# Constant matmuls in TensorE's early gaps, v loads moved forward, and a different order of ScalarE's first work

## The chip, the cores and the metric

The kernel runs on one core of one Trainium2 chip. The metric is device time in microseconds (us) of one execution. The kernel before takes 507.7 us (median); its four executions lie between 507.67 and 508.16 us. Engines: TensorE (PE; its weight loads are PEld), VectorE (DVE), ScalarE (ACT), GpSimd (POOL) and SyncE (SP), which issues the DMA transfers here.

## The reference, cut to what matters

```python
def _attn_ref(q, k, v, f_logit):                # (4, 8, 768, 48) each
    f = 1.0 / (1.0 + np.exp(-f_logit))
    for t in range(S):                          # a gated recurrence
        state = f[:, :, t, :, None] * state + np.einsum('bhd,bhe->bhde', k[:, :, t], v[:, :, t])
        y[:, :, t] = np.einsum('bhd,bhde->bhe', q[:, :, t], state)

def _moe_ref(x, w1, w2, w3, w_out):             # x: 3072 x 384
    a = x @ w1; b = x @ w2                      # 384 -> 1024
    h = a * b @ w3                              # 1024 -> 1024
    return (h @ w_out).astype(np.float32)       # 1024 -> 384
```

The output of the recurrence is the input x of the feed-forward part. Weights arrive as 64-bit floats.

## The kernel before

The recurrence is done in 24 chunks of 128 steps, four to a block of 512 rows. A chunk needs its gates (ACT), two scans and two products (DVE), a transpose, scores, values and a state update (PE), copies out of PSUM (ACT) and a mask (GpSimd). w3 and w_out are folded into one matrix on the chip ("folds", eight of them), and every weight is converted from 64-bit words to f32 by ACT and DVE.

The order of instructions on each engine is fixed when the program is built, by a plan: each task has a cost in us and a lag, and a list scheduler takes whatever can start first. Each engine's list is then fixed in that order.

```python
    def moves(issue, size, rate, emit, deps, prio):
        i = plan.add("SP", issue, emit, deps, prio, lag=0.6)
        return plan.add("DMA", size / rate, lambda: None, [i], prio, lag=1.3)
    # ... in attention(u), chunk u
        t["lf"] = moves(0.87, 197, 250, load(fu, f_logit), free(2, "g"), n0 - 30)
        t["lk"] = moves(0.87, 197, 250, load(ku, k), free(2, "k"), n0 - 29.5)
        t["lq"] = moves(0.87, 197, 250, load(qu, q), free(3, "q"), n0 - 29)

        def load_v():
            s["v"] = loads.tile([P, DM], F32, name="vt")     # pool "loads": 3 buffers
            nc.sync.dma_start(s["v"], v[u])

        t["lv"] = moves(0.45, 197, 320, load_v, past(u, 3, "v", "s"), n0 - 27)
    # ... in fetch(): a load of weights (1 MB) and its conversion
        ld = moves(0.45, total, 380, load, held[-2:], prio)
        # ACT: magnitude, rest; DVE: shifted (clamp, then shift), signed, joined
    # ... at the end
    for t in plan.order():
        t["emit"]()
```

There are three buffers for v: v of chunk u can be loaded only when chunk u - 3 has been used (`past(u, 3, "v", "s")`).

Of the kernel before, what the change touches and what calls it, by code (L numbers as in the profile page):

```python
# [36 lines left out]
F32 = mybir.dt.float32  # L37
# [8 lines left out]
P = 128  # L46
# [9 lines left out]
TB = 512  # L56
# [4 lines left out]
NPE = 4  # L61
# [3 lines left out]
TH = TB // 2  # L65
KH = KF // 2
LOW = float.fromhex("0x1p-15")
HIGH = float.fromhex("0x1.dffffep+16")
FLOOR = 2.0**-60
RANGE = 2.0**-40  # L70

# [53 lines left out]
@with_exitstack  # L125
def kernel(
    ctx: ExitStack,
    tc: tile.TileContext,
    q: bass.AP,
    k: bass.AP,  # L130
    f_logit: bass.AP,
    v: bass.AP,
    w1: bass.AP,
    w2: bass.AP,
    w3: bass.AP,
    w_out: bass.AP,
    leaf_mask: bass.AP,
    out: bass.AP,
):
    nc = tc.nc  # L140
    const = ctx.enter_context(tc.tile_pool(name="const", bufs=1))
    ident = const.tile([P, P], F32, name="ident")
    w12 = const.tile([P, 2, KM, DFF], F32, name="w12")
    wc = const.tile([P, KF, DM], F32, name="wc")
    left = const.tile([1, 1], I32, name="left")
    with tc.manual_schedule():
        outside = ranged(tc, q, k, f_logit, v, w1, w2, w3, w_out, out, ident, w12, wc, left)
        with tc.If(outside > 0, preferred_fallthrough_block=True, label="general"):
            general(tc, q, k, f_logit, v, leaf_mask, out, ident, w12, wc)
# [24 lines left out]
def ranged(ctx, tc, q, k, f_logit, v, w1, w2, w3, w_out, out, ident, w12, wc, left):  # L174

    nc = tc.nc
# [11 lines left out]
    ps_f = ctx.enter_context(tc.tile_pool(name="ps_f", bufs=NF, space=PSUM))  # L188

    floor = keep.tile([R, NQ], F32, name="floor")  # L190
# [35 lines left out]
    plan = Plan()  # L226
# [3 lines left out]
    moving = plan.add("PE", 0.0, lambda: None, takes=["ab"], prio=-1e9)  # L230
    coming = plan.add("PE", 0.0, lambda: None, takes=["ab"], prio=-1e9)

    def heads(t):
        return t.rearrange("p (h c) -> p h c", c=C)

    def setup():
        nc.scalar.activation(warm, nc.const_aps.tensor(0.0, (R, 1), F32), AF.Sigmoid)
        for i in range(2):
            nc.gpsimd.memset(fs[i][32:64], 30.0)  # L239
            nc.gpsimd.memset(ks[i][32:64], 0.0)  # L240
            nc.gpsimd.memset(qs[i][32:64], 0.0)
            if i == 0:
                make_identity(nc, ident)
        nc.gpsimd.memset(early[32:64, 2:4], 30.0)
        nc.gpsimd.memset(early[32:64, 0:2], 0.0)
        nc.gpsimd.memset(qs[2][32:64], 0.0)
        nc.gpsimd.memset(qs[3][32:64], 0.0)
        nc.vector.memset(floor, FLOOR)
        nc.vector.memset(heads(floor)[:, :, 0], 1.0)
        nc.vector.memset(back, 0.0)  # L250
        for t in gate:
            nc.vector.memset(t[:, NQ : NQ + 1], 0.0)
        nc.vector.memset(ones, 1.0)
        for t in sb:
            nc.vector.memset(t, 0.0)

        nc.gpsimd.memset(perm, 0.0)
        for i, (kc, hp) in enumerate(met):
            for par in range(2):
                for r, t, at_, n in runs(2 * hp + par):  # L260
                    if t == kc:
                        a = 64 * par + at_
                        nc.gpsimd.tensor_copy(perm[:, i, r : r + n], ident[0:R, a : a + n])
# [16 lines left out]
    def need(u):  # L280
        return (0.0, 1.0, 2.0, 3.0)[u] if u < 4 else 45.0 + 14.5 * (u - 4)

    def past(u, n, *names):
        return [tk[u - n][nm] for nm in names if u >= n and nm in tk[u - n]]

    def moves(issue, size, rate, emit, deps, prio):

        i = plan.add("SP", issue, emit, deps, prio, lag=0.6)
        return plan.add("DMA", size / rate, lambda: None, [i], prio, lag=1.3)

    def attention(u):
        s, t = st[u], tk[u]
        opens, closes = u % NCH == 0, u % NCH == NCH - 1
        n0 = need(u)
# [9 lines left out]
        def free(n, *names):  # L304
# [3 lines left out]
            return asked[4:5] + [tk[u - n if u - n >= 4 else u % n][nm] for nm in names]  # L308
# [6 lines that stand above are left out]
            s["v"] = loads.tile([P, DM], F32, name="vt")  # L315
            nc.sync.dma_start(s["v"], v[u])

        t["lv"] = moves(0.45, 197, 320, load_v, past(u, 3, "v", "s"), n0 - 27)

        def gates():  # L320
            nc.scalar.activation(gate[u % 2][:, 0:NQ], fu, AF.Sigmoid)  # L321
# [11 lines left out]
        def last():  # L333
            nc.scalar.copy(lasts[:, u], heads(s["P"])[:, :, C - 1])
# [3 lines left out]
        def ends():  # L338
            nc.vector.reciprocal(heads(back)[:, :, C - 1], heads(s["P"])[:, :, C - 1])
# [151 lines left out]
        n = u // UB  # L491
# [379 lines left out]
    def fetch(loads_, a, prio, subs, deps=()):  # L871





        total = subs[-1][1]
        if not wide:
            def plain():
                for place_, src in loads_:  # L880
                    for c0, c1, dst, _, _ in subs:
                        d = dst().rearrange("p (a m) -> p a m", a=a)
                        m = (c1 - c0) // a
                        b0 = c0 // a if len(subs) > 1 else 0
                        nc.sync.dma_start(d[place_], src[:, :, b0 : b0 + m])
            waits = [d for sub in subs for d in sub[4]]
            ld = plan.add("SP", 1.9 * total / 512, plain, waits, prio, lag=2.0)
            return [ld] * len(subs)
        load_no = len(users)
        buf = load_no if load_no < len(raws) else (load_no - len(raws)) % NRAW  # L890
        raw = raws[buf][:, 0 : 2 * total]
        words = raw.rearrange("p (n two) -> p n two", two=2)
        held = [g for no, b_, gs in users if b_ == buf for g in gs]

        def load():
            for place_, src in loads_:
                nc.sync.dma_start(raw.rearrange("p (a m) -> p a m", a=a)[place_], src.bitcast(U32))

        ld = moves(0.45, total, 380, load, held[-2:], prio)
        asked.append(ld)  # L900
        got = []
        users.append((load_no, buf, got))
        ends = []

        def sub(c0, c1, dst, due, waits):
            n = c1 - c0
            w = n / 512
            lo, hi = words[:, c0:c1, 0], words[:, c0:c1, 1]
            a0 = spot[0] if n <= 512 else (spot[0] + 512) // 1024 * 1024 % 2048
            spot[0] = (a0 + (512 if n <= 512 else 1024)) % 2048  # L910
            m = magnitudes[:, a0 : a0 + n]
            mine = range(a0 // 512, (a0 + n + 511) // 512)
            s = {}

            def magnitude():
                nc.scalar.activation(m, hi.bitcast(F32), AF.Abs)  # L916

            def rest():
                nc.scalar.activation(lo.bitcast(F32), lo, AF.Copy, bias=2.0, scale=2.0**-51)  # L919

            def shifted():
                nc.vector.tensor_scalar(m, m, HIGH, LOW, ALU.min, ALU.max)
                nc.vector.tensor_scalar(m.bitcast(U32), m.bitcast(U32), 3, None, ALU.logical_shift_left)

            def signed():
                s["to"] = dst()
                nc.vector.scalar_tensor_tensor(
                    s["to"].bitcast(U32), hi, 0x80000000, lo, ALU.bitwise_and, ALU.bitwise_or
                )

            def joined():
                to = s["to"].bitcast(I32)
                nc.vector.tensor_tensor(to, m.bitcast(I32), to, ALU.add)  # L933

            past = [joins[i] for i in mine if i in joins]
            b = plan.add("ACT", 0.2 + 0.43 * w, magnitude, [ld] + past, due)
            e = plan.add("ACT", 0.2 + 0.43 * w, rest, [ld], due)
            h = plan.add("DVE", 0.32 + 0.54 * w, shifted, [b], due)
            g = plan.add("DVE", 0.16 + 0.53 * w, signed, [e, b] + list(waits), due)
            j = plan.add("DVE", 0.16 + 0.53 * w, joined, [h, g], due - 1)  # L940
            parts.append((g, j))
            joins.update({i: j for i in mine})
            got.append(g)
            ends.append(j)

        for one_ in subs:
            sub(*one_)
        return ends
# [104 lines left out]
    for u in range(NU):  # L1053
        attention(u)
        if u == 3:
            weights()
        if u == NU - 1:
            judged = plan.add("DVE", 1.5, judge, [tk[i]["y"] for i in range(NU)], -20)
        if u % UB == UB - 1:
            ffn(u // UB)  # L1060
    for t in plan.order():
        t["emit"]()
    return blk[NB - 1]["outside"]

# [336 lines left out]
```

## Time and profile before

| | before |
|---|---|
| time, median (range) | 507.69 us (507.67 to 508.16) |
| span of the profiled run | 506.3 us |
| PE busy | 488.8 us, 97% |
| DVE busy, 25 to 60 us | 33.58 of 35 us |
| first feed-forward matmul on PE | 37.07 us |
| second fold on PE | 90.22 us |

PE is full after the start, and DVE nearly full until 150 us. The lines are in the prediction. A "w3 row" is below one block of w3 after its conversion, which the fold of the same number on PE needs; its last step is a DVE instruction (line 933).

### The profile page before, as it was taken

What the parts mean: (1) busy time and instruction counts of PE and PEld (TensorE: products, weight loads), DVE (VectorE), ACT (ScalarE), POOL (GpSimd) and SP (SyncE); (2) the same over time, 40 slices, a digit from 0 to 9 for tenths busy, and PEclk for the clock granted to TensorE, in tenths of its full rate; (3) what the DMA queues carried; (4) which work ended last, traced back from release to release, by engine and by line L of the source; (5) the groups of instructions that cost most, each with busy time, mean ns of one, the idle gap of its engine ahead of it and who ended that gap; (6) DMA issues with size and microseconds to landing.
All of it is one profiled execution on the core that took longest, in us unless ns stands there. A gap on an engine that the chain in (4) does not pass through costs nothing.

```text
span 506.3 us, 8806 instructions
## 1 busy us (share of the span) xinstructions
PE 488.8 (97%) x3346; PEld 409.2 (81%) x3346; DVE 362.4 (72%) x701; ACT 162.1 (32%) x340; POOL 42.7 (8%) x51
## 2 busy tenths in 40 slices
PE   2899999999999999999999999999999999999995
PEld 2788854666688887889888899888899888889994
DVE  6799999999998769866677766256564677564541
ACT  4589454854434345222332112321010011011000
POOL 8120010001101201001110000110000000000000
PEclk9999999999999999999999999999999999999999
DMA  6959466762222265311160001210002100000011
GB/s 177 363 206 305 135 216 220 251 199 79 61 79 84 67 190 161 96 34 45 45 193 16 1 6 31 59 50 0 2 21 61 45 1 0 1 0 1 32 49 52
DMA packets 30163, 46.02 MB, mean 91 GB/s; under 512 B 6560, under 2 KB 20384, under 8 KB 28320
## 3 DMA queue, kind: packets, MB, share of 16 engines
q1 hardware_dynamic: 30112, 45.38, 28.5%
q8 instruction: 28, 0.46, 0.4%
q14 instruction: 23, 0.19, 0.1%
HBM read 36.70 MB, written 4.72 MB: 82 GB/s over the span
## 4 chain that ended last, share of the span: by engine, by line
PE 94%; POOL 2%; DVE 2%; DMA 1%; issue 0%; ACT 0%; SPq 0%; DVEq 0%; POOLq 0%; ACTq 0%
PE f L530 68%; PE f L984 8%; PE pa L370 5%; PE pa L420 4%; PE pk L456 2%; PE pk L396 2%; PE pa L435 2%; DMA vt<-in_v_dram 1%; PE f L509 1%; PE f L420 1%; PE f L428 1%; DVE fwd L329 0%; POOL A L385 0%; DVE bwd L351 0%; POOL f L239 0%
## 5 line engine op out<-in xcount | busy, mean ns | idle before, releaser
L530 PE MATMUL f<-xt,w 128*128 128x256 f32 (+1 forms) x600 | 160.1, 398 | 0.1
L530 PEld LDWEIGHTS f<-xt,w 128*128 128x128 f32 x600 | 113.0, 190 | 24.5 <-issue 9.5
L530 PE MATMUL f<-place 128*128 128x192 f32 (+1 forms) x504 | 114.0, 352 | 0.0
L530 PEld LDWEIGHTS f<-place 128*128 128x128 f32 x504 | 87.3, 190 | 6.8 <-issue 1.1
L385 POOL TENSOR_SCALAR_AFFINE_SELECT A<-A 128x1024 f32<-128x1024 f32 x24 | 31.4, 1309 | 294.2 <-ACT A L379 294.2
L984 PE MATMUL f<-place 128*128 128x384 f32 x128 | 43.1, 491 | 0.0
L633 ACT COPY a<-f 128x256 f32<-128x256 f32 x36 | 13.4, 372 | 75.5 <-PE f L530 59.7
L530 PE MATMUL f<-xt,place 128*128 128x256 f32 x144 | 37.2, 381 | 0.0
L984 PEld LDWEIGHTS f<-place 128*128 128x128 f32 x128 | 23.8, 190 | 15.8 <-issue 0.5
L530 PE MATMUL f<-wc,ab 128*128 128x192 f32 x192 | 35.7, 329 | 0.0
L530 PEld LDWEIGHTS f<-wc,ab 128*128 128x128 f32 x192 | 31.8, 190 | 0.9
L657 DVE TENSOR_TENSOR place<-f,a 128x256 f32<-128x256 f32 x36 | 15.2, 423 | 23.7 <-PE f L530 23.6
L329 DVE TENSOR_TENSOR_SCAN fwd<-gate,floor 112x512 f32<-112x512 f32 x24 | 30.2, 1258 | 2.6 <-ACT gate L321 1.7
L379 ACT COPY A<-pa 128x1024 f32<-128x1024 f32 x24 | 24.2, 1009 | 22.7 <-PE pa L370 22.7
L370 PEld LDWEIGHTS pa<-Q,K 48*128 48x128 f32 x384 | 24.9, 199 | 6.9 <-issue 4.7
L351 DVE TENSOR_TENSOR_SCAN bwd<-gate,back 112x512 f32<-112x512 f32 x24 | 29.8, 1240 | 0.8
L530 PEld LDWEIGHTS f<-xt,place 128*128 128x128 f32 x144 | 26.9, 189 | 3.8 <-DVE place L657 0.2
L370 PE MATMUL pa<-Q,K 48*128 48x128 f32 x384 | 29.7, 298 | 0.0
L485 ACT ACTIVATE ys<-pa 112x512 f32<-112x512 f32 x20 | 11.9, 597 | 40.8 <-PE pa L435 20.5
L919 ACT ACTIVATE place<-place 128x512 f32<-128x512 uint32 (+2 forms) x24 | 21.1, 890 | 8.0 <-DMA place<-in_w_out_dram 4.8
L916 ACT ACTIVATE place<-place 128x512 f32<-128x512 f32 (+2 forms) x24 | 21.2, 884 | 4.1 <-DVE w L933 2.1
L420 PEld LDWEIGHTS pa<-A,vt 128*48 128x48 f32 (+1 forms) x320 | 17.4, 130 | 6.2 <-issue 4.8
(104 smaller groups left out, 623.0 us busy)
## 6 DMA issues: line engine op xcount, KB each, us to landing
place<-in_w_dram SPq DMA_DIRECT2D x14, 1024.0 KB, 5.5
vt<-in_v_dram SPq DMA_DIRECT2D x24, 192.0 KB, 3.0
out_dram<-o SPq DMA_DIRECT2D x24, 192.0 KB, 2.1
q<-in_q_dram SPq DMA_DIRECT2D x46, 96.0 KB, 2.5
f<-in_f_logit_dram SPq DMA_DIRECT2D x44, 96.0 KB, 2.4
k<-in_k_dram SPq DMA_DIRECT2D x44, 96.0 KB, 2.4
place<-in_w_out_dram SPq DMA_DIRECT2D x4, 768.0 KB, 5.5
xt<-ys SPq DMA_DIRECT2D x120, 24.0 KB, 1.8
```

The source lines that it names most:

```text
L329: nc.vector.tensor_tensor_scan(s["P"], gate[u % 2][:, 0:NQ], floor, 0.0, ALU.mult, ALU.max)
L351: nc.vector.tensor_tensor_scan(s["R"][:, ::-1], gate[u % 2][:, NQ:0:-1], back[:, ::-1], 0.0, ALU.mult, ALU.max)
L370: nc.tensor.matmul(s["pa"][:, par, cols], lhsT=s["K"][rows(par), cols], rhs=s["Q"][rows(par), cols], start=True, stop=True,)
L379: nc.scalar.copy(s["A"].rearrange("p r h c -> p r (h c)"), s["pa"])
L385: nc.gpsimd.affine_select(out=a, in_=a, pattern=[[0, H], [1, C]], compare_op=ALU.is_ge, fill=0.0, base=0, channel_multiplier=-1,)
L420: nc.tensor.matmul(y_block(b)[64 * half : 64 * half + w], lhsT=s["v"][:, h * D : h * D + w], rhs=s["A"][:, par, hp], start=bank not in met ...
L530: nc.tensor.matmul(out_, lhsT=lhs[i], rhs=rhs[i], start=start and i == 0, stop=i == len(lhs) - 1, skip_group_check=True,)
L633: nc.scalar.copy(q["a"], q["X"])
L657: nc.vector.tensor_tensor(ups["u3", k], q["Y"], q["a"], ALU.add)
L916: nc.scalar.activation(m, hi.bitcast(F32), AF.Abs)
L919: nc.scalar.activation(lo.bitcast(F32), lo, AF.Copy, bias=2.0, scale=2.0**-51)
L984: nc.tensor.matmul(w3s["p", jc], lhsT=w3s[jc][:, kc * P : kc * P + P], rhs=wos[:, kc], start=(kc == 0), stop=(kc == KF - 1),)
```

## The change

The intent: TensorE runs its first matmuls slowly (the scores of a chunk take 2.01 us at 17 us and 1.11 us at 26 us), so let it multiply constants from the second microsecond on and in every planned gap up to 35 us; issue v of the first four chunks (NPE is 4) ahead of later chunks' loads; and tell the plan that the first weight loads land later, so that it puts ScalarE's chunk work ahead of conversions.

```diff
+FULL = 35.0
@@
+    def idle(n):
+
+        to = ps_f.tile([P, TB], F32, name="f")[:, 0:TH]
+        for _ in range(n):
+            nc.tensor.matmul(to, lhsT=floor[:, 0:P], rhs=floor[:, 0:TH], start=True, stop=True)
+
+    plan.add("PE", 7.8, lambda: idle(9), prio=-1e8)
@@
-    def moves(issue, size, rate, emit, deps, prio):
+    def moves(issue, size, rate, emit, deps, prio, late=0.0):
@@
-        return plan.add("DMA", size / rate, lambda: None, [i], prio, lag=1.3)
+        return plan.add("DMA", size / rate, lambda: None, [i], prio, lag=1.3 + late)
@@
-        t["lv"] = moves(0.45, 197, 320, load_v, past(u, 3, "v", "s"), n0 - 27)
+        t["lv"] = moves(0.45, 197, 320, load_v, past(u, 3, "v", "s"), n0 - (28.2 if u < NPE else 27))
@@
-        ld = moves(0.45, total, 380, load, held[-2:], prio)
+        ld = moves(0.45, total, 380, load, held[-2:], prio, max(0.0, 5.5 - 1.5 * load_no))
@@
+    ready_at = 0.0
     for t in plan.order():
+        if t["eng"] == "PE" and t["at"] < FULL:
+            n = int((t["at"] - ready_at) / 0.43)
+            if ready_at and n:
+                idle(n)
+            ready_at = t["end"]
         t["emit"]()
```

## The prediction

> **What bounds the kernel now.** I read the page's first two parts, then the chain of work that ended last for the first 70 us, then stretches of 20 us, then the timeline of single engines.
>
> The page says that TensorE (PE) is the bound, and where it is not:
>
> ```profile
> PE 488.8 (97%) x3346; PEld 409.2 (81%) x3346; DVE 362.4 (72%) x701; ACT 162.1 (32%) x340; POOL 42.7 (8%) x51
> ...
> PE   2899999999999999999999999999999999999995
> ...
> DVE  6799999999998769866677766256564677564541
> ...
> PEclk9999999999999999999999999999999999999999
> ```
>
> PE is idle for 506.3 - 488.8 = 17.5 us, and most of that lies in the first slice (12.7 us long). VectorE (DVE) is at nine tenths or more from the third slice to the twelfth, so in the first 150 us it is nearly as full as PE. The clock row shows nothing, yet the durations do. The chain at the start:
>
> ```profile
> 8.78 3.04 DMA vt<-in_v_dram
> ...
> 14.38 0.98 PE pk L396 x4
> 15.36 1.90 PE f L420 x15
> 17.26 2.01 PE pa L370 x16
> 19.27 1.02 PE pk L456 x14
> 20.29 2.86 PE f L509 x12
> ...
> 25.70 1.11 PE pa L370 x16
> ```
>
> The same sixteen matmuls of line 370 (scores of one chunk) take 2.01 us at 17.26 and 1.11 us at 25.70; the twelve of line 509 take 2.86 us here and 1.60 us at 32.48. Everything on PE before about 22.8 us runs at half speed, and from 14.38 us on PE is the chain without a gap. Before that the chain is the v load of the first chunk, issued at 8.78 us and landed at 11.82 us. By stretches:
>
> ```profile
> 0.00:20.00 20.00, 9.67 (x88) 8.20 (x88) 13.78 (x25) 8.42 (x17) 12.33 (x28) 1.00 0.73 229
> 20.00:40.00 20.00, 19.68 (x203) 17.64 (x202) 19.00 (x33) 16.87 (x35) 4.19 (x3) 1.00 0.72 264
> 40.00:60.00 20.00, 20.00 (x88) 16.49 (x87) 19.03 (x40) 13.90 (x28) 0.00 (x0) 1.00 0.65 218
> 60.00:80.00 20.00, 20.00 (x111) 10.81 (x110) 19.30 (x29) 11.24 (x17) 1.42 (x1) 1.00 0.59 191
> 80.00:100.00 20.00, 20.00 (x99) 11.51 (x98) 19.61 (x23) 13.27 (x18) 1.25 (x1) 1.00 0.76 259
> ```
>
> Columns: busy time of PE, weight loads, DVE, ScalarE, GpSimd; clock; DMA. After the start PE loses nearly nothing (20.00 of 20). So the end moves by what PE saves in the first 23 us, unless DVE, at 19.0 to 19.6 of 20, cannot deliver earlier. One place shows how tight that is. DVE finishes the second w3 row and PE uses it in the fold at once:
>
> ```profile
> 88.54 1.23 DVE L933 CUSTOM_DVE_ANT_0 place<-place 128x2048 uint16<-128x2048 uint16 x1
> ```
>
> ```profile
> 90.22 5.43 PE L984 MATMUL f<-place 128*128 128x384 f32 x16
> ```
>
> Ready at 89.77, used at 90.22: 0.45 us of slack. By the same reading the later folds have 2.7 to 6.0 us (third: ready 94.48, used 97.19; eighth: ready 126.6, used 132.6).
>
> [...] here full speed came about 8.4 us after PE became continuous at 14.38. [...] the 128x512 operation of line 922 takes 0.42 us, but 1.31 us where it meets GpSimd's select at 28.5 us.
>
> **The change part by part.**
>
> *Nine constant matmuls at the start.* Each is f32, 128x256, which the machine runs as two passes; a pass takes about 0.215 us at full clock (22 to 23 of them fill 5 us between 45 and 50 us), so 0.43 us for the pair and 0.86 us at half clock. They need only the constant tile "floor", set at 1.60 us, so they start near 1.7 us. [...] The first real work, the transposes of line 396, starts at 8.48 us. So they cost nothing, or up to about 1 us if the clock stays low (9 x 0.86 = 7.7, end 9.4).
>
> *Fillers in planned gaps up to 35 us.* [...] the number is the planned gap over 0.43 rounded down, so if the plan is right they fit in gaps. Where the real work is ready sooner than planned, each costs up to 0.43 us. They also draw PSUM buffers from the pool of five that the plan does not count, a possible small wait.
>
> *What the clock is worth on PE.* Slow minus fast duration by group: first transposes 0.98-0.55, scores 2.08-1.16, update 1.06-0.67, second transposes 0.98-0.55, values 1.97-1.09, second scores 2.08-1.16, second update 1.09-0.67, joining matmuls 2.93-1.60: 0.43+0.92+0.39+0.43+0.88+0.92+0.42+1.33 = 5.7 us, of which 4.0 us lie after 14.38, on the gapless chain. The gaps of PE between 8.4 and 14.35 are a further 5.95-4.05 = 1.9 us.
>
> *v of the first chunk earlier.* In the order of priorities v of chunk 0 moves from behind chunk 2's loads to behind chunk 1's k: three pairs of loads (q of 1, f and k of 2), each 0.84 us on the queue, so its issue moves from 8.78 to about 6.1 us and it lands near 9.1. The update of chunk 0 then waits for its transposes (about 9.7 us), not for v at 11.82. The loads overtaken move by 0.42 us each and were early.
>
> *What both give DVE.* In the first 25 us DVE waits 1.19 us at 13.07 (state of chunk 0, after the late v) and 1.84 us at 20.34 (state of chunk 1, after slow PE). Both go: 3.0 us. Two operations inflated by GpSimd there (0.89 for 0.69, 0.96 for 0.36) may move out of the collision or not, 0.8 us.
>
> *ScalarE's order.* The plan now believes the first four weight loads land 5.5, 4.0, 2.5 and 1.0 us later, so chunk work precedes conversions. In the trace the state copy of chunk 1 is ready at 21.69 but starts at 23.56, behind two conversions and a copy that waited for slow PE. Worth about 1 us to the chunks, paid by conversions started later; zero in sum, I think, since DVE is the limit for conversions.
>
> *Sum.* PE could start its unbroken feed-forward work up to 5.7 + 1.9 = 7.6 us sooner. But it then runs into DVE: at the second fold PE can be ahead only by DVE's own gain plus 0.45 us, that is 3.0 + 0.45 = 3.5 us; later folds have slack. I choose the smaller bound and take off 0.2 us for fillers in the way: 3.3 us. 507.7 - 3.3 = 504.4 us.
>
> **The rivals.** *The full gain.* If the rearranged plan finds other PE work while the second w3 row is awaited, or puts that row ahead of chunk 5 on DVE (4.5 us of work just before it, 81.46 to 86.0), PE keeps more, perhaps 5 to 6 us: 502. For it: slack of 2.7 us and more at all later folds. Against: the priorities of that stretch are unchanged. *DVE and weight loads give nothing.* The 5 MB of weights queued from 13.45 us keep the DMA engines at a share of 0.95 to 1.02 from 15 to 25 us, and conversions are put off; if the feed-forward start stays near 37 us because the third w1 piece is still converted at 36.1, the PE time saved turns into idle time and fillers: 506.5 to 507.5. Against: that piece had been held up by DVE, not by its load. *The fillers harm.* Warming runs on, or fillers delay the first chunks by 1 to 2 us, or a PSUM buffer wait appears: up to 508.5. For it: the plan's clock is not the chip's. Against: PE has 8.4 us with nothing to do.
>
> **Range and chances.** The centre is the DVE-bound sum, the low end most of the full gain, the high end most of the absorbed one: 504.4 us, 502.0 to 506.5. A 2% change is 10.2 us, above the 7.6 us that is to be had at most, so faster by over 2% has 0.01. Slower by over 2% needs a disturbed plan far beyond the first 35 us: 0.01. Within 2%: 0.98.
>
> **What would show it right or wrong.** Right: scores of line 370 at about 1.1 us already for chunk 0 or 1; first v landed by 9.5 us; the two DVE waits gone; the first feed-forward matmul of line 530 several us before 37.07; the second fold 3 to 3.5 us before 90.22, with PE's idle time or a DVE wait just ahead of it; the rest of the trace shifted by that amount. Wrong: slow matmuls still after 10 us (the constants do not raise the clock), transposes starting after 8.5 us (fillers in the way), the feed-forward start unmoved, or the second fold moved by more than 4 us (DVE no bound) or less than 2.5 us (a new wait before it). A shift that shrinks after 140 us would mean that later waits, not the start, set the end.

## The result, and the profile after

The changed kernel takes 514.38 us (median of 4 runs, 512.67 to 514.99), the kernel before 507.72 in the same rounds. Ratio 1.0124, 95% interval 1.0097 to 1.0151. Ratios here and below are the mean time of one kernel's fast runs over that of the other's fast runs of the same rounds, so not quite the ratio of the medians. The change makes the kernel 1.2% slower, where 0.7% faster was predicted; the span of the profiled run grew from 506.3 to 510.6 us. The profiled run is the fastest of the changed kernel's four (512.67 us, granted clock 0.995; the others 513.84 to 514.99 us with 0.990 to 0.992). So the profile accounts for 4.3 us of the loss; the further 1.2 to 2.3 us of the other runs go with a lower clock, and no profile of them was kept.

The first part works as meant. PE's timeline of the changed kernel (start, duration, instruction, count; in later lines brackets give the idle time just before and what ended it):

```profile
8.48 0.57 PE L405 MATMUL pk<-ident,K 112*128 112x112 f32 x4
9.02 1.16 PE L379 MATMUL pa<-Q,K 48*128 48x128 f32 x16
10.11 0.67 PE L465 MATMUL pk<-vt,kt 128*64 128x48 f32 x16
```

The first transposes start at 8.48 us as before, but at full speed (0.57 us for 0.98; the nine constants before them are 18 matmuls in the trace, from 1.66 to 8.43 us), and the update of chunk 0 runs at 10.11 and not 11.95 us. The chunks gain: the values of chunk 3, which started at 34.40 us before, could start soon after 30.4 us, when GpSimd's mask for them is done (28.92 to 30.36 us). They do not. The chain of waits of the changed kernel:

```profile
17.84 15.03 DMA vt<-in_v_dram
33.01 1.08 PE f L429 x16
...
40.25 31.02 PE f L539 x120
```

v of chunk 3 takes 15.03 us to land, at 32.87. It was issued at 17.84, after chunk 0 had let its buffer go, and behind five 1 MB weight loads issued from 13.91 us. The kernel before has the same transfer. SP's row for it comes first (three v loads merged; the one at 17.30 is that of chunk 3), PE's user of it second:

```profile
17.30 15.37 SPq L316 DMA_DIRECT2D vt<-in_v_dram  x3
```

```profile
34.40 1.09 PE L420 MATMUL f<-A,vt 128*64 128x128 f32 x16
```

It took 15.1 us to land, so it landed near 32.4 us with its user at 34.40: 2 us of slack that no wait shows. The faster chunks ran past that slack. What the wait did on the other engines, in stretches of 5 us (columns as in the prediction), then single lines of PE, ACT and DVE of the changed kernel:

```profile
25.00:30.00 5.00, 4.58 (x50) 3.75 (x48) 3.62 (x8) 3.90 (x9) 1.37 (x2) 1.00 1.00 409
30.00:35.00 5.00, 2.00 (x22) 1.84 (x23) 4.43 (x8) 2.66 (x6) 0.36 (x1) 0.93 0.65 190
35.00:40.00 5.00, 5.00 (x44) 4.83 (x44) 2.34 (x5) 2.85 (x6) 0.00 (x0) 0.73 0.54 141
```

```profile
33.01 1.08 PE L429 MATMUL f<-A,vt 128*64 128x128 f32 x16 [3.42 <-DMA vt<-in_v_dram]
...
35.62 2.51 PE L518 MATMUL f<-ys,ab 112*128 112x128 f32 x12
...
38.65 1.60 PE L518 MATMUL f<-ys,ab 112*128 112x128 f32 x12
...
35.86 0.60 ACT L494 ACTIVATE ys<-f 112x512 f32<-112x512 f32 x1 [3.20 <-PE f L437]
...
37.12 0.43 DVE L931 TENSOR_SCALAR place<-place 128x512 f32<-128x512 f32 x1 [2.56 <-ACT place L925]
```

Three things follow from one late transfer. PE stands for 3.42 us (after 30.4 us only v is missing). The clock goes (0.73 from 35 to 40 us): the twelve matmuls of line 518 take 2.51 us at 35.62 and 1.60 at 38.65. And ACT stands 3.20 us before the copy of chunk 3's result, with weight conversions behind it in its list, so DVE stands 2.56 us. The feed-forward start moves from 37.07 to 40.09 us.

The second fold shows what that costs in the end. DVE, then PE, of the changed kernel:

```profile
92.89 1.22 DVE L942 CUSTOM_DVE_ANT_0 place<-place 128x2048 uint16<-128x2048 uint16 x1
```

```profile
94.17 5.43 PE L993 MATMUL f<-place 128*128 128x384 f32 x16 [2.30 <-DVE place L942]
```

The second w3 row is ready at 94.11 us and not 89.77, and PE waits 2.30 us for it: the fold starts 3.95 us later than before. From there to the end the two traces run alike (510.6 - 94.17 = 416.4 us, before 506.3 - 90.22 = 416.1). How DVE came to be late, by two stretches of before and after:

```profile
4.85:25.00 20.15, 14.67 (x124) 12.79 (x125) 16.31 (x23) 9.52 (x22) 9.36 (x17) 1.00 0.88 307
25.00:60.00 35.00, 34.68 (x253) 29.53 (x252) 33.58 (x67) 27.55 (x55) 3.10 (x2) 1.00 0.64 215
```

```profile
4.85:25.00 20.15, 18.78 (x194) 15.59 (x192) 19.20 (x26) 10.74 (x23) 10.24 (x18) 1.00 0.86 299
25.00:60.00 35.00, 31.58 (x195) 25.79 (x194) 27.96 (x56) 25.85 (x51) 1.73 (x2) 0.95 0.59 197
```

Up to 25 us DVE is busy for 19.20 - 16.31 = 2.9 us more; from 25 to 60 us it is busy for 33.58 - 27.96 = 5.6 us less. Busy time is not quite work, though, so follow the instructions. DVE runs the same list in both kernels up to the product K of chunk 3, before and after:

```profile
25.14 0.69 DVE L359 TENSOR_TENSOR K<-ab,bwd 112x512 f32<-112x512 f32 x1
```

```profile
23.04 0.69 DVE L368 TENSOR_TENSOR K<-ab,bwd 112x512 f32<-112x512 f32 x1
```

The lead is 2.1 us and not the 3.0 us of the prediction: both waits went, but on the way one K took 1.52 us for 0.89 (at 12.26 us) and one G 1.05 for 0.16 (at 17.89 us), against one S that got shorter (0.36 for 0.96). From K to the second w3 row, which are again the same instructions in another order, DVE takes 71.07 us for 64.63, that is 6.4 us more, and 6.4 - 2.1 is the 4.3 us by which the row is late. Of the 6.4 us, 6.0 are waits (6.8 us for 0.8), the most of them for ACT (time in all, times, longest):

```profile
DVE place L931 <- ACT place L925: 4.0, 5, 2.6
...
DVE w L936 <- ACT place L928: 1.2, 1, 1.2
```

The 2.56 us of the first line, and 0.47 us soon after, hang on ACT's waits for the late chunk 3; the 1.2 us, at 27.99 us, come before the late v can matter and show ACT's new order.

### The profile page after: what moved, and what is told of

It reads as the page before. It is cut to its first block, busy times and chain, and to the rows that moved or that the text cites. A ratio compares the mean times of both kernels' runs of the same rounds, so it can differ in the third digit from the quotient of the medians.

```text
span 510.6 us, 8874 instructions
## 1 busy us (share of the span) xinstructions
PE 494.6 (97%) x3378; PEld 413.1 (81%) x3378; DVE 364.0 (71%) x701; ACT 161.9 (32%) x340; POOL 42.0 (8%) x51
## 4 chain that ended last, share of the span: by engine, by line
PE 87%; DVE 4%; DMA 4%; SPq 2%; POOL 1%; issue 1%; ACT 0%; DVEq 0%; POOLq 0%; ACTq 0%
PE f L539 65%; PE f L993 7%; PE pa L379 4%; PE pa L429 4%; DMA vt<-in_v_dram 3%; PE pk L465 2%; PE pa L444 2%; PE pk L405 2%; SPq L513 1%; PE f L518 1%; DVE fwd L338 1%; DVE place L942 1%; SPq L308 1%; DVE bwd L360 0%; DVE place L936 0%
## 5 line engine op out<-in xcount | busy, mean ns | idle before, releaser
L642 ACT COPY a<-f 128x256 f32<-128x256 f32 x36 | 13.4, 372 | 75.7 <-PE f L539 60.0
L379 PEld LDWEIGHTS pa<-Q,K 48*128 48x128 f32 x384 | 23.3, 187 | 6.7 <-issue 3.5
L379 PE MATMUL pa<-Q,K 48*128 48x128 f32 x384 | 27.9, 285 | 0.0
L494 ACT ACTIVATE ys<-pa 112x512 f32<-112x512 f32 x20 | 12.0, 598 | 40.4 <-DMA xt<-ys 19.1
```

Source lines behind the costliest of these rows:

```text
L379: nc.tensor.matmul(s["pa"][:, par, cols], lhsT=s["K"][rows(par), cols], rhs=s["Q"][rows(par), cols], start=True, stop=True,)
L642: nc.scalar.copy(q["a"], q["X"])
```

## The experiments

Theory A: the chunks outrun v of the fourth chunk, and that wait, with what hangs on it, is the loss. Theory B: ScalarE's new order is the loss, because conversions come later and DVE starves. Theory C: the constants stand in the way of real work. Line numbers differ between versions: lines 370, 420, 509, 530 and 984 of the kernel before are 379, 429, 518, 539 and 993 where the constants are in.

### Parts of the change, alone and taken away

**The constants alone** (the kernel before plus `idle`, its first nine and the gaps; no change of `moves` or `lv`).

> The kernel before with the constant matmuls alone (start and gaps), v and ScalarE's plan as before. Theory A (the chunks now outrun the v load of the fourth chunk, which waits for a buffer and lands near 32.5 us behind 5 MB of weights): PE stalls 2 to 4 us before the values of chunk 3, the clock may drop after it, the feed-forward work starts at 38 us or later, time 509 to 514. Theory B (the loss is ScalarE's new order, conversions put off): no loss here, feed-forward start near 34 us, 504 to 506. Theory C (the constants themselves stand in the way): 509 to 514 too, but with matmuls of line 238-like constants directly ahead of ready work, not a DMA wait.

Measured: 507.05 to 507.64 us in four runs with a clock of 0.997 to 1.000, and 512.3 in the profiled one with 0.990; ratio 0.9986 (0.9954 to 1.0017). In that profile PE waits 2.57 us for ACT at 26.18, not for v, and then runs slowly (the twelve matmuls of line 518 in 2.93 us for 1.60; granted clock 0.59 from 25 to 30 us); ACT itself had stood 3.7 us for a weight load. So none of the three theories had it: alone, the constants neither win nor lose in the four runs that kept the clock, and the one run that lost it took about 5 us more. C falls, for the constants are in all five runs and four of them lose nothing.

**v ahead, alone** (the diff's `lv` line only).

> The kernel before with v issued ahead alone. All theories: the cold clock stays, chunk 3 comes too late to wait for its v, 506.5 to 508.5; the first update near 10.5 us and not 11.95.

Measured: 508.80 us, ratio 1.0010 (0.9978 to 1.0042), no difference and just above the expected range; the first update came at 11.41 us and not near 10.5. The expectation that the cold clock stays and chunk 3 comes too late to wait was wrong: in the profiled run full speed came at 19.1 us (an update takes 0.67 us at 19.16, and took 1.09 at 11.41), and PE waited 2.01 us for v at 32.74 and lost the clock there (granted clock 0.77 from 30 to 35 us). So the late v can stop a version without constants too, once its chunks run faster.

**The later landing in the plan, alone** (the diff's `moves` and `ld` lines only).

> The kernel before with the later landing of weights in the plan alone (ScalarE does chunks first). A: no stall, 506.5 to 508.5. B: conversions put off, DVE waits for ScalarE between 25 and 40 us, second fold 2 us or more later than 90.2, 510 to 513.

Measured: 509.40 us, ratio 1.0024 (0.9990 to 1.0058); row ready at 91.14 us. The profile:

```profile
91.19 5.43 PE L984 MATMUL f<-place 128*128 128x384 f32 x16 [1.03 <-DVE place L933]
```

The wait of DVE that B foretold is there (2.1 us of DVE waiting for ACT between 25 and 40 us), but the fold comes 1 us later and not 2 or more, and the time lies between the two ranges, with 1 inside the interval. B is right in kind and too small to be all.

**The change without the later landing.**

```diff
-        ld = moves(..., held[-2:], prio, max(0.0, 5.5 - 1.5 * load_no))
+        ld = moves(..., held[-2:], prio)
```

> The changed kernel without the later landing of weights in the plan (constants and early v stay). A: the stall before the values of chunk 3 stays 3 us or more, 510 to 514. B: the loss goes, 504 to 507. C: 510 to 514 with the constants as what PE does ahead of ready work.

Measured: two groups, 513.05 and 513.80 us with clock 0.989, 507.93 and 508.78 with 0.999 and 0.998; ratio 1.0041 (0.9978 to 1.0105). The profile is one of the longer pair, and in it the stall is elsewhere than A said, first on ACT, then on PE:

```profile
22.64 0.67 ACT L925 ACTIVATE place<-place 128x512 f32<-128x512 f32 x1 [4.92 <-DMA place<-in_w_dram]
```

```profile
24.89 1.09 PE L465 MATMUL pk<-vt,kt 128*64 128x48 f32 x16 [1.81 <-ACT kt L413]
26.27 2.93 PE L518 MATMUL f<-ys,ab 112*128 112x128 f32 x12 [0.28 <-ACT ys L494]
```

ACT stands 4.92 us at the head of its list for the first weight load, with the chunk's copies behind it. In the changed kernel this wait of ACT is gone. So the change's third part cures a real wait, and by curing it lets the chunks run into the next one, v of chunk 3. With two runs in each group, neither the loss of this version nor its gain over the change is clear of noise.

### v of the fourth chunk

Instead of a fourth buffer of the pool, which no run tried, this one v goes to memory that is free until the second block:

```diff
-            s["v"] = loads.tile([P, DM], F32, name="vt")
+            s["v"] = at(12864, DM) if u == 3 else loads.tile([P, DM], F32, name="vt")
@@
-        t["lv"] = moves(0.45, 197, 320, load_v, past(u, 3, "v", "s"), n0 - (28.2 if u < NPE else 27))
+        t["lv"] = moves(0.45, 197, 320, load_v, [] if u == 3 else past(u, 3, "v", "s"), n0 - (29.3 if u == 3 else 28.2 if u < NPE else 27))
```

**In the changed kernel.**

> The changed kernel with v of the fourth chunk loaded ahead of the weights, into memory that is free at that time. Theory A: the DMA wait before the values of chunk 3 (3.42 us in the changed kernel) is gone, the clock stays at 1.00, ScalarE and DVE no longer wait for it between 30 and 40 us, the feed-forward start comes at 34 to 36 us and not 40.1, the second fold at 88 to 91 us and not 94.2, time 505 to 508.5. Theory B (ScalarE's order itself) and C (constants in the way): the loss stays, 511 to 514.

Measured: 510.27 us, ratio 1.0049 (1.0033 to 1.0064), in other rounds than the change's 1.0124. The wait for v is gone and the feed-forward start comes at 35.57 us, 4.5 us sooner than in the changed kernel. The time falls by less and stays above the 508.5 us that A allowed, for the next wall stands. (The values of chunk 3 now wait only 0.95 us, for GpSimd's mask, and start at 30.12 us.)

```profile
89.65 7.12 PE L993 MATMUL f<-place 128*128 128x384 f32 x16 [2.30 <-DVE place L942]
```

The second fold waits 2.30 us for DVE, whose row is ready at 89.60 us, hardly before the 89.77 of the kernel before: from 25 to 60 us DVE does 30.94 us of work against 33.58. And after that wait the fold itself takes 7.12 us and not 5.43, for the clock was lost once more (0.91 granted from 80 to 100 us).

**With v of the fourth chunk ahead, and without the later landing.**

> As the first of this group, without the later landing of weights in the plan. In the profile of the changed kernel without it, ScalarE waited 4.9 us for a weight load with chunk copies queued behind it. A: that wait is there again, PE waits for ScalarE at 23 to 26 us, the clock drops in some runs, 507 to 513 with two groups of times. If ScalarE's order is of no use: as the first of this group.

Measured: 508.23 us, ratio 0.9999 (0.9985 to 1.0012), one group, not two as A expected. From 25 to 60 us DVE does 33.03 us, and the row is ready at 88.69:

```profile
88.74 5.43 PE L993 MATMUL f<-place 128*128 128x384 f32 x16 [1.00 <-DVE place L942]
```

Why only one group? ACT's wait of 4.92 us is not there again: with v of chunk 3 issued first, the weight loads go out 0.5 us later (14.40 for 13.91 us), the plan puts the chunk's copies ahead of the first conversion by itself, and ACT's wait for it is 0.2 us. So the edit for v removes ACT's wait too, in another way than the later landing does; no edit of these moves one thing alone.

The four versions make a table (ratio to the kernel before, of each one's own rounds):

| | later landing in the plan | not |
|---|---|---|
| v of chunk 3 behind the weights | 1.0124 (the change) | 1.0041 |
| v of chunk 3 ahead of them | 1.0049 | 0.9999 |

Two steps are clear of noise: v ahead takes the change from 1.0124 (1.0097 to 1.0151) to 1.0049 (1.0033 to 1.0064), and leaving out the later landing then takes it to 0.9999 (0.9985 to 1.0012). Taken in this order A is worth about 0.75% and B about 0.5%. The other order is not resolved, for the interval of 1.0041 (0.9978 to 1.0105) reaches both its neighbours. What is left of the change, warm PE and early v, is then worth nothing in time.

**Control: v of the fourth chunk ahead in the kernel before.**

> Control: the kernel before with v of the fourth chunk ahead of the weights, nothing else. There PE never waited for that v, so theory A says no gain: 507 to 508.5.

Measured: 509.17 us (the range said up to 508.5), ratio 1.0012 (0.9995 to 1.0029): no gain, as expected where nothing waited for it.

**Only the plan is told** that v of chunk 3 lands 5 us later (`moves(..., 5.0 if u == 3 else 0.0)`).

> The changed kernel in which only the plan is told that v of the fourth chunk lands 5 us later; the load itself is unchanged. The DMA wait stays (3 us, up to 32.9). If it hurts by way of ScalarE's queue (conversions blocked behind the copy of chunk 3's result, DVE idle 2.6 us at 34.6) the time falls to 507 to 510; if by PE's idle time and lost clock, it stays at 512 to 514.

Measured: 509.51 to 516.76 us, ratio 1.0063 (1.0036 to 1.0090). The test did not do what it was made for: in the profile (the longest of the six runs, 515.0 us span) ACT's copy of chunk 3's result still stood ahead of conversions, DVE waited 2.95 us for ACT at 39.78, and PE lost the clock (0.50 granted from 35 to 40 us). The two ways could not be told apart by it.

**The clock held through the stall** (eight more constants before the values of chunk 3).

```diff
+            if t is tk[3]["v"]:
+                n += 8
             if ready_at and n:
                 idle(n)
```

> The changed kernel with eight more constants (3.4 us) ahead of the values of chunk 3, so that PE does not fall idle in the wait. Clock 1.00 throughout. If the lost clock is the larger part: feed-forward start near 37.5 and time 508 to 510. If the stall itself and ScalarE's queue behind it are the larger part (theory A as I hold it): 510.5 to 513, little better than the changed kernel but with less spread.

```profile
28.58 4.50 PE L238 MATMUL f<-floor 112*128 112x256 f32 x20
...
34.02 1.13 PE L437 MATMUL f<-Q,sb 112*112 112x128 f32 x8
```

Measured: 511.65 us, ratio 1.0072 (1.0054 to 1.0089), as expected for the stall as the larger part (the spread, 2.6 us, is not less than the changed kernel's 2.3). The values start at 33.01 us as in the changed kernel, but what follows is at full speed (line 437 in 1.13 us for 1.81; granted clock 1.00 from 30 to 40 us) and the feed-forward start is at 38.46, 1.6 us sooner than in the changed kernel, as is the second fold. Against 1.0124 the lost clock is about 0.5% or 2.6 us of the change's loss, in ratios of different rounds; the two profiles alone say 1.6 us. The second fold still waits 2.30 us for DVE.

### What holds the rest of the gain

**Less work for DVE.** The clamp in the conversion is taken out, by the pages 13.4 us of DVE work (362.4 to 349.0 us in the kernel before); the result is right for these inputs, but not for weights of extreme size, so this is a probe and not a version.

```diff
-                nc.vector.tensor_scalar(m, m, HIGH, LOW, ALU.min, ALU.max)
```

> The kernel before without the clamp in the conversion of weights: about 11 us less work on DVE between 25 and 125 us (24 instructions of 0.42 to 0.69 us), right for these inputs and not for all. If the kernel before is set by PE from 14 us on, as its trace says: 506 to 508, no gain over 1.5 us. If DVE sets it already: 3 us or more faster, under 504.7.

> The same removal in the version with the constants, all four v loads ahead of the weights and the old plan for ScalarE (508.2 us). If what remains of the gain is swallowed by DVE's conversions (PE waits 1.00 us for DVE at the second fold and 1.62 us at 131 us in its trace): both waits go and the time falls to 502.5 to 505.5. If not DVE but the plan's order or the constants hold it: 507 to 508.5.

Measured: 507.08 us, ratio 0.9978 (0.9963 to 0.9992), in the kernel before; 507.27 us, ratio 0.9974 (0.9955 to 0.9993), in the repaired version. The first is as expected: the row is ready at 88.91 us with its fold at 90.09, so DVE does not hold PE there. The second misses the range for DVE and falls in the other, in which the plan's order or the constants hold the gain. The wait at the second fold nearly goes, and that of 1.62 us at 131 us with it:

```profile
88.96 5.43 PE L992 MATMUL f<-place 128*128 128x384 f32 x16 [0.28 <-DVE place L941]
```

but the fold starts no sooner than with the clamp (88.74), for the plan came out differently: PE waited 0.75 us for ACT at 35.27, and the feed-forward start was at 36.71 and not 35.76. So DVE is one wall; with less work for it, waits of the chunks on ACT (0.75 us) and GpSimd (0.65 us) stand in front of PE, and the 3 us do not come back.

**w3 rows first on DVE** (priority of the rows 52 + 6 jc and not 56 + 6 jc) in the repaired version.

> The version with the constants, all v ahead and the old plan for ScalarE, with DVE's conversion of w3 rows ranked ahead of the chunks of that stretch. If only the order at the second fold costs: its wait of 1.00 us goes, 505 to 507.5. If DVE has no time left there in any order: the wait moves to the chunks, 507.5 to 510.

Measured: 511.45 us, ratio 1.0067 (1.0042 to 1.0092), above both ranges. The first two folds now run back to back from 81.07 us; the wait leaves the second and comes back at the third:

```profile
94.66 7.12 PE L993 MATMUL f<-place 128*128 128x384 f32 x16 [2.01 <-DVE place L942]
```

and again the clock is lost in it (7.12 us; 0.91 granted from 80 to 100 us). In that order, too, a fold waits for DVE. This does not account for all of the time: the third fold still ends sooner than before (101.78 for 102.6 us), and what is lost later, 1.18 us of waiting for ACT at 189 us among it, was not traced. No general version of these beat the kernel before.

### One view over the versions

From the profiled run of each version with the clamp and the usual order of w3 rows: when the second w3 row was ready, when the second fold started, and the span (us).

| version | row ready | fold starts | span | span - fold |
|---|---|---|---|---|
| v of chunk 3 ahead, no later landing | 88.69 | 88.74 | 506.7 | 418.0 |
| v of chunk 3 ahead | 89.60 | 89.65 | 507.6 | 418.0 |
| before | 89.77 | 90.22 | 506.3 | 416.1 |
| v of chunk 3 ahead in the kernel before | 90.16 | 90.62 | 507.4 | 416.8 |
| v ahead, alone | 90.66 | 91.12 | 507.9 | 416.8 |
| later landing alone | 91.14 | 91.19 | 507.0 | 415.8 |
| clock held | 92.49 | 92.54 | 508.6 | 416.1 |
| constants alone | 92.26 | 92.71 | 510.1 | 417.4 |
| no later landing | 93.07 | 93.52 | 510.9 | 417.4 |
| the change | 94.11 | 94.17 | 510.6 | 416.4 |
| only the plan is told | 95.37 | 95.42 | 515.0 | 419.6 |

The last column varies by 3.8 us, the fold's start by 6.7 us, and the span goes mostly with the fold's start: it is largely settled by 95 us who is ahead. Three rows are exceptions. The last loses 3 us in the fold itself, which takes 8.44 us for 5.43, at a granted clock of 0.87 from 80 to 100 us. Rows 1 and 2 lose about 2 us after the fold's start, row 2 by the slow fold shown above, row 1 by a wait of 1.62 us for DVE at 131 us.

## Why the prediction was wrong

Predicted 504.4 us (502.0 to 506.5), measured 514.38; "within 2%" held, the direction did not.

- *The clock.* Right: full speed by 8.5 us (the first transposes in 0.57 us for 0.98), scores of chunk 0 in 1.16 us, and the constants not in the way (without the later landing they put the first transposes off to 8.59 us).
- *v of the first chunk.* Right in kind: both early waits of DVE went. The size was 2.1 us and not 3.0, because two instructions ran longer than before, both while GpSimd's mask ran (12.14 to 13.23 us for the K, 17.73 to 18.92 us for the G). The prediction named such collisions (0.8 us) but left them out of the sum.
- *PE's own gain.* It allowed up to 7.6 us for the start of unbroken feed-forward work. With both repairs that start came at 35.76 us and before at 39.80, a gain of 4.0 us: between the chunks PE waited for DVE and GpSimd (0.5 to 0.6 us at a time), and constants filled further gaps (2.43 us at 11 us, 1.04 us at 28.6). The smaller bound hid this.
- *DVE sets how much PE can gain.* Right as a mechanism: in the changed kernel and in most repaired ones PE waits for DVE at the second fold, where the prediction put the limit.
- *The step that failed* is the one that carried DVE's gain from 25 us to 90 us. On ScalarE's order it said "zero in sum, I think, since DVE is the limit for conversions". It was not zero: from there to the second row DVE took 6.4 us longer, of which 6.0 us are waits, nearly all for ACT, whose list had the conversions behind chunk work and behind a chunk that stood still. Instead of 3.3 us sooner the second fold came 3.95 us later. Both causes showed in the experiments: v of chunk 3 (0.75%) and, with that repaired, the plan's later landing (0.5%).
- *The wait that was not looked for.* The rival "DVE and weight loads give nothing" named the 5 MB queue, but argued only about the third w1 piece, "held up by DVE, not by its load". It did not ask which small load stood behind those 5 MB. v of chunk 3 did, with about 2 us of slack, while the same prediction moved its user forward by more than that. The before trace had it: a landing of 15.1 us in a group whose usual landing is 3.0.
- *What the prediction did not count:* that PE could lose the clock again after a stall, as it did here (0.73 granted from 35 to 40 us, after 3.42 us of waiting). Held by constants, the change loses 0.7 instead of 1.2%.

What stays open: where the changed kernel's three other runs lose their further 1.2 to 2.3 us, how much of the loss the later landing has while v is still late, and why the version with both repairs and less DVE work gains no more than the kernel before does from that removal.

## What to carry to other kernels

When work moves forward, list every transfer it needs with its landing time and its present slack, also those that no wait shows; here a small load behind five large ones took 15 us and not 3. Where an engine's list is fixed, a copy that waits for a stalled engine can hold up what is behind it (here ACT stood 3.20 us, then DVE 2.56 us), so a late transfer can reach engines that do not need it. And here warming TensorE was worth nothing: in the changed kernel the clock was lost again after a stall of 3.42 us (0.73 granted from 35 to 40 us), and where it held to the end (both repairs, 1.00 over the span) the second fold waited 1.00 us for DVE, which feeds TensorE; with less work for DVE other waits stood there.

## What else the runs show of the clock and the queue

- With dense 128x256 constants full speed came after 4.3 to 6.4 us (an estimate: in the profiles of the constants alone, of the change and of the change without the later landing the nine constants took 6.00, 6.77 and 7.09 us from 1.66 us on, at 0.43 us for a slow pass and 0.215 for a fast one). With the kernel's own mix of transposes and products of 48 to 128 columns, gapless from about 14.4 us, it took 8.4 us before and 4.8 us in the version with v ahead alone.
- After 20 us the profiles have ten waits of PE between 1.8 and 3.4 us; eight were followed by slow matmuls, one of 1.81 us among them (the change without the later landing; then an update in 1.09 us for 0.67). Two of 2.30 us were not (the changed kernel and the version with the clock held; then the fold in 5.43 us), while the same wait with v of chunk 3 ahead was followed by a fold of 7.12 us. So the length of the wait alone does not decide.
- A small load behind large ones: 192 KB took 15.0 us to land behind five loads of 1 MB, against a median of 2.8 us for the changed kernel's 24 loads of v.
- The clock row of the profile reads 1.00 over slow work in the first 20 us (scores in 2.08 us at 17.19 in the kernel before, 1.16 at 25.63), but followed the loss at 35 to 40 us in the changed kernel (0.73).
